# All AV runs of a batch behind its last scores, three row-tiled token blocks in the second GEMM, and a first GEMM that opens in the score banks

## The chip, the core and the metric

The kernel runs on one core of one Trainium2 chip. The metric is the time of one execution in device microseconds (us), and what is compared is the median of several executions. One further execution is recorded by the hardware profiler; all durations of single instructions come from that one.

## What is computed

A causal attention with forget gates, followed by an MLP with the exact GELU, both for 8 batches of 576 tokens with 8 heads of width 64. Cut to what matters:

```python
scores = q @ k.T / sqrt(64) + decay            # decay from cumsum(log f), causal mask
attn   = exp(scores - max); attn /= attn.sum(-1)
x      = (attn @ v)  -> [4608, 512]            # heads side by side
h      = x @ w_in                              # w_in  [512, 2048]
g      = 0.5 * h * (1 + erf(h / sqrt(2)))
out    = g @ w_out                             # w_out [2048, 512]
```

## The kernel before

The order of the work on every engine is written out by hand: each engine runs its instructions in the order in which the code issues them, and waits at an instruction for the semaphores of those on other engines. The waits themselves are placed by the framework, tile by tile: an instruction that writes a tile waits for the earlier readers of that tile.

**One batch.** A batch b from 2 to 7 is `attention(b)` (line 824) and then the rest of its first GEMM (lines 951 to 980). Its parts are these.

- Scores. For each of 4 head pairs i and each of 4 score tiles t, `scores(b, i, t)` (line 299) makes q times k for two heads at once. The matmuls have 64 rows of contraction, so the two heads run side by side in the two row halves of the array. ScalarE (ACT) takes the exponential of the tile from PSUM into an SBUF tile e (line 329), and GpSimd (POOL) masks the diagonal (line 331). The tiles t hold 448, 384, 448 and 320 columns for each head.
- Fill. Between the scores the PE works on the second GEMM of the batch before: `gemm2_rows` (line 489) is a generator of 64 steps, 16 for each of 4 blocks of 128 tokens, and `take(fill, n)` runs n of them. A step "n" is one matmul with 128 rows. A step "r" is row-tiled: two matmuls of 64 rows that run side by side, into two PSUM banks that VectorE (DVE) adds up later (a copy at line 517 and an addition at line 529, in `sum_out`). `PLAN` (line 472) says for each block which PSUM pool it takes and which steps are "r"; `FILL` (line 821) says how many steps follow each score tile.
- AV. `av(i)` (line 830) runs, for each of the two heads, 15 matmuls with 128 rows and 65 columns (line 350) into one bank of the pool "o", then `normalize` on DVE (a reciprocal at line 363 and a multiplication at line 364, from that bank into the SBUF tile x). When both heads are done, `x_dma` (line 388) has SyncE (SP) issue a DMA that transposes x into xT, the input of the first GEMM.
- First GEMM. `gemm1(b, ffb, kts, ps)` (line 400) adds the contraction parts kts (0 to 3, one for each head pair) of block ffb of 16 into the bank ps. With part 3 it issues `gelu`, an ACT instruction at line 425 that reads the bank.

**PSUM** has 8 banks: the pool "s" has two tiles of two banks each (the score tiles), "o" two tiles of one bank, "m" two tiles of one bank. Each pool hands its tiles out in turn.

**The order around the change**, for b of 3 to 7. `FILL` puts 7, 6, 3, 3 steps behind the four tiles of pair 0, and so on, 48 in the loop. `av(0)` and `av(1)` run inside the loop, behind the second tile of pairs 1 and 2 (line 842). After the loop come `av(2)`, 3 steps, `av(3)` with one step between its heads, the addition of block 2 that was put off (line 862), and the last 12 steps. Then the first GEMM opens:

```python
pss = [gemm1(b, ffb, (0, 1)) for ffb in range(2)]             # banks of "m"
for ffb in range(2):
    gemm1(b, ffb, (2,), pss[ffb])
pss += [gemm1(b, ffb, (0, 1, 2), spare()) for ffb in (2, 3)]  # banks of "o"
for ffb in range(4):
    gemm1(b, ffb, (3,), pss[ffb])                             # and a gelu each
more = s_psum.tile([P, 2, 512], FP32, tag="s", name="ps1")
gemm1(b, 4, ps=more[:, 0, :])
```

Blocks 5, 6 and 9 to 15 follow in banks of "m", blocks 7 and 8 in banks of "o". The other place where two blocks of the first GEMM share one tile of "s" is `gemm1_begin` (line 802), for batch 1; there the gelus of these two blocks are issued behind the last matmul of both (lines 814 to 817).

SP's queue of a batch holds, in this order: two transposing loads of the next batch's q and k, five loads of v, the store of token block 0, two more transposing loads, and then the `x_dma` of the four pairs with the stores of blocks 1 to 3 between and behind them.

Of the kernel before, what the change touches and what calls it, by code (L numbers as in the profile page):

```python
# [2 lines left out]

# [6 lines left out]
FP32 = mybir.dt.float32  # L10
# [5 lines left out]
P = 128  # L16
# [3 lines left out]
HP = 4  # L20
# [34 lines left out]
def kernel(  # L55
# [16 lines left out]
    n_ff = d_ff // P  # L72
# [11 lines left out]
    h_pool = ctx.enter_context(tc.tile_pool(name="h", bufs=1))  # L84
    e_pool = ctx.enter_context(tc.tile_pool(name="e", bufs=4))
    tq_pool = ctx.enter_context(tc.tile_pool(name="tq", bufs=1))
    x_pool = ctx.enter_context(tc.tile_pool(name="x", bufs=3))
    xT_pool = ctx.enter_context(tc.tile_pool(name="xT", bufs=2))
    g_pool = ctx.enter_context(tc.tile_pool(name="g", bufs=2))
    o_pool = ctx.enter_context(tc.tile_pool(name="outs", bufs=4))  # L90
    s_psum = ctx.enter_context(tc.tile_pool(name="s_psum", bufs=2, space=PSUM))
# [251 lines left out]
    def attend(b, i, h, ms, pool=o_psum, tag="o"):  # L343
        if (b, i, h) not in o_of:
            o_of[b, i, h] = pool.tile([P, NBLK, D + 1], FP32, tag=tag, name="o")
        o = o_of[b, i, h]
        for m in ms:
            for n in range(m + 1):
                t, c = where(n, m)
                nc.tensor.matmul(  # L350
                    o[:, m, :],
                    e_of[b, i, t][:, h, c : c + P],
                    vw_of[b][:, 2 * i + h, n, :],
                    start=(n == 0),
                    stop=(n == m),
                )

    def normalize(b, i, h):
        if (b, i) not in x_of:
            x_of[b, i] = x_pool.tile([P, NBLK, 2, D], BF16, tag="x", name="x")  # L360
        o = o_of[b, i, h]
        r = x_pool.tile([P, NBLK], FP32, tag="r", name="r")
        nc.vector.reciprocal(r, o[:, :, D])  # L363
        nc.vector.tensor_tensor(  # L364
            x_of[b, i][:, :, h, :],
            o[:, :, 0:D],
            r.unsqueeze(2).to_broadcast([P, NBLK, D]),
            Alu.mult,
        )

    def xT(b):
        if b not in xT_of:
            xT_of[b] = xT_pool.tile([P, n_dm, XC], BF16, tag="xT", name="xT")
        return xT_of[b]
# [25 lines left out]
    def gemm1(c, ffb, kts=range(4), ps=None, act=True):  # L400
        src = xT(c) if c < B else tails
        if ps is None:
            ps = m_psum.tile([P, TC], FP32, tag="m", name="ps1")
        for kt in kts:
            nc.tensor.matmul(  # L405
                ps,
                w_in_sb[:, kt, ffb * P : (ffb + 1) * P],
                src[:, kt, 0:TC],
                start=(kt == 0),
                stop=(kt == n_dm - 1),  # L410
            )
        if n_dm - 1 in kts and act:
            gelu(c, ffb, ps)
        return ps

    def spare():
        return o_psum.tile([P, TC], FP32, tag="o", name="ps1")

    def gelu(c, ffb, ps):
        if c not in g_of:  # L420
            g_of[c] = [
                g_pool.tile([P, TC], BF16, tag=f"g{n}", name=f"g{n}")
                for n in range(n_ff)
            ]
        nc.scalar.activation(g_of[c][ffb], ps, Act.Gelu)  # L425
# [9 lines left out]
    def gemm2(c):  # L435
# [35 lines left out]

    PLAN = [
        (0, "o", 16 * "r"),
        (1, "m", 6 * "r" + "n" + 7 * "r" + 2 * "n"),
        (2, "m", 16 * "r"),
        (3, "s", 16 * "n"),
    ]

    PLAN_0 = [(2, "o", 16 * "r"), (3, "m", 14 * "r" + 2 * "n")]
# [3 lines left out]
        (2, "m", 12 * "r" + 4 * "n"),  # L483
        (3, "s", 16 * "n"),
    ]

    put_off = []

    def gemm2_rows(c, plan):

        for ts, held, steps in plan:
            if held == "s":
                both = s_psum.tile([P, 2, d_model], FP32, tag="s", name="ps2")
                banks = [both[:, 0], both[:, 1]]
            else:
                pool = {"o": o_psum, "m": m_psum}[held]
                banks = [  # L500
                    pool.tile([P, d_model], FP32, tag=held, name="ps2")
                    for _ in range(2)
                ]
            ot = o_pool.tile([P, d_model], FP32, tag="ot", name="ot")
            for kt, step in enumerate(steps):
                last = kt == steps.rfind("r")
                for r in range(2 if step == "r" else 1):
                    rows = slice(r * D, (r + 1) * D) if step == "r" else slice(0, P)
                    nc.tensor.matmul(  # L509
                        banks[r],  # L510
                        g_of[c][kt][rows, ts * P : (ts + 1) * P],
                        w_out_sb[rows, kt, :],
                        start=kt == (steps.index("r") if r else 0),
                        stop=last if r else kt == n_ff - 1,
                    )
                if "r" in steps and (kt == n_ff - 1 if held == "s" else last):
                    nc.vector.tensor_copy(ot, banks[1])  # L517
                if kt == n_ff - 1:
                    if plan is PLAN and ts == 2:
                        put_off.append(partial(sum_out, c, ts, ot, banks[0]))  # L520
                    elif "r" in steps:
                        sum_out(c, ts, ot, banks[0])
                    else:
                        nc.vector.tensor_copy(ot, banks[0])
                        store(c, ts, ot)
                yield

# [53 lines left out]
    def gemm2_third():  # L581
        yield from gemm2_second(0)
        yield from gemm2_rows(0, PLAN_0)
        yield from gemm2_rows(1, PLAN_1)

    def take(gen, n):
        for _ in range(n):
            if next(gen, "end") == "end":
                return
# [228 lines left out]

    FILL = [[7, 6, 3, 3], [1, 3, 3, 3], [1, 2, 3, 3], [3, 2, 3, 2]]
    FILL_2 = [[8, 8, 8, 8], [8, 8, 4, 4], [4, 4, 4, 4], [4, 4, 4, 4]]

    def attention(b):


        fill = gemm2_third() if b == 2 else gemm2_rows(b - 1, PLAN)
        counts = FILL_2 if b == 2 else FILL

        def av(i, n=0):  # L830
            for h in range(2):
                attend(b, i, h, (0, 1, 2, 3, 4))
                normalize(b, i, h)
                if h == 0:
                    take(fill, n)
            x_dma(b, i)

        for i in range(HP):
            for t in range(4):
                scores(b, i, t)  # L840
                take(fill, counts[i][t])
                if t == 1 and 0 < i < (HP if b == 2 else HP - 1):
                    av(i - 1)
                    if b == 2 and i == 1:
                        load_v(3)
                if b == 2 and (i, t) == (0, 3):
                    weigh_v(b, 2)
                    weigh_v(b, 3)
                if b > 2 and i == 0 and t == 1:
                    load_v(b + 1)  # L850
                if b > 2 and t == 0 and i < 2:
                    transpose_dma(b + 1, 4 * i, 4 * i + 4)
                if b == 2 and t == 1 and i == 1:
                    transpose_dma(3, 0, 4)
        if b == 2:
            take(fill, 4)
            av(HP - 1)
        else:
            av(HP - 2)
            take(fill, 3)  # L860
            av(HP - 1, 1)
            put_off.pop()()
        take(fill, 4)
        if b == 2:
            transpose_dma(3, 4, 8)
        take(fill, 999)

        pss = [gemm1(b, ffb, (0, 1)) for ffb in range(2)]
        for ffb in range(2):
            gemm1(b, ffb, (2,), pss[ffb])  # L870
        pss += [gemm1(b, ffb, (0, 1, 2), spare()) for ffb in (2, 3)]
        for ffb in range(4):
            gemm1(b, ffb, (3,), pss[ffb])
        more = s_psum.tile([P, 2, 512], FP32, tag="s", name="ps1")
        gemm1(b, 4, ps=more[:, 0, :])
        if b + 1 < B:
            untangle(b + 1, 0)
            weigh_v(b + 1, 0)
        x_tail(b)
# [135 lines left out]
```

## Time and profile before

| | |
|---|---|
| median of 3 executions | 334.37 us (333.99 to 334.4) |
| the profiled execution | 335.58 us, of which the span of the profile is 333.8 us |
| PE (matmuls) busy | 325.1 us, 97% of the span |
| ACT busy | 205.5 us, 62% |
| DVE busy | 184.2 us, 55% |
| POOL busy | 134.2 us, 40% |
| DMA | 44.18 MB, mean 132 GB/s |
| batches 3 to 7 | 34.8 to 34.9 us each, of a span of 333.8 us |

The profile is of the one execution that has 335.58 us. PE means the matmuls and PEld the weight loads that run beside them. Matmuls are pipelined: the row of a 512-column matmul says 379 ns, but the next one starts some 216 ns after it. A group is named by line, engine, operation and tiles (out<-in), with the busy time and the mean time of one in ns. The chain of waits is the work that ended last, followed back from the end, each piece with its start and its length in us. The timeline gives start, length, engine, line and the number of instructions of a merged piece, and in brackets how long the engine was idle before it and for what it waited.

### The profile page before, as it was taken

What the parts mean: (1) busy time and instruction counts of PE and PEld (TensorE: products, weight loads), DVE (VectorE), ACT (ScalarE), POOL (GpSimd) and SP (SyncE); (2) the same over time, 40 slices, a digit from 0 to 9 for tenths busy, and PEclk for the clock granted to TensorE, in tenths of its full rate; (3) what the DMA queues carried; (4) which work ended last, traced back from release to release, by engine and by line L of the source; (5) the groups of instructions that cost most, each with busy time, mean ns of one, the idle gap of its engine ahead of it and who ended that gap; (6) DMA issues with size and microseconds to landing.
All of it is one profiled execution on the core that took longest, in us unless ns stands there. A gap on an engine that the chain in (4) does not pass through costs nothing.

```text
span 333.8 us, 8055 instructions
## 1 busy us (share of the span) xinstructions
PE 325.1 (97%) x3287; PEld 170.1 (51%) x3287; DVE 184.2 (55%) x427; ACT 205.5 (62%) x296; POOL 134.2 (40%) x260
## 2 busy tenths in 40 slices
PE   8899999999999999999999999999999999999995
PEld 4664555445554466445644565455544654444443
DVE  5852657474549855894589547954795450010011
ACT  4786886974535786478736892788278836405600
POOL 8897873039327054704472354534442420000000
PEclk9999999999999999999999999999999999999999
DMA  7899999989999899389939895889700420021022
GB/s 118 192 202 218 206 194 98 195 170 156 206 195 179 133 219 157 92 136 175 209 111 141 160 174 157 115 153 212 155 1 3 100 75 33 0 89 38 0 50 77
DMA packets 94948, 44.18 MB, mean 132 GB/s; under 512 B 74176, under 2 KB 89792, under 8 KB 94912
## 3 DMA queue, kind: packets, MB, share of 16 engines
q1 hardware_dynamic: 77760, 27.16, 42.6%
q0 software_dynamic: 16752, 15.99, 30.7%
q8 instruction: 25, 0.41, 0.5%
q10 hardware_dynamic: 400, 0.52, 0.4%
q14 instruction: 11, 0.09, 0.1%
HBM read 36.85 MB, written 9.44 MB: 139 GB/s over the span
## 4 chain that ended last, share of the span: by engine, by line
PE 95%; ACT 2%; DVE 1%; issue 1%; DVEq 0%
PE ps L405 37%; PE ps L509 27%; PE ps L449 8%; PE o L350 8%; PE s L319 7%; PE s L619 1%; PE ps_w L210 1%; PE ps_f L226 1%; ACT e L624 1%; PE ps L569 1%; PE ps L545 1%; PE o L650 0%; ACT e L329 0%; PE ps_x L383 0%; DVE x L664 0%
## 5 line engine op out<-in xcount | busy, mean ns | idle before, releaser
L425 ACT ACTIVATE g<-ps 128x512 bf16<-128x512 f32 x138 | 78.5, 602 | 79.5 <-PE ps L405 78.9
L405 PE MATMUL ps<-xT,w_in_sb 128*128 128x512 bf16 x512 | 114.1, 379 | 0.1
L509 PE MATMUL ps<-w_out_sb,g 64*128 64x512 bf16 (+1 forms) x711 | 108.5, 377 | 0.0
L329 ACT ACTIVATE e<-s 128x896 bf16<-128x896 f32 x112 | 87.7, 836 | 21.3 <-PE s L319 18.8
L405 PEld LDWEIGHTS <-w_in_sb 128*128 128x128 bf16 x576 | 55.3, 98 | 66.6 <-issue 2.6
L331 POOL TENSOR_SCALAR_AFFINE_SELECT e<-e 128x256 bf16<-128x256 bf16 (+1 forms) x135 | 49.1, 383 | 87.5 <-ACT e L329 87.1
L509 PEld LDWEIGHTS <-g 64*128 64x128 bf16 (+1 forms) x711 | 40.2, 95 | 34.8 <-issue 4.7
L288 POOL TENSOR_TENSOR vw<-v_sb,wT 128x640 bf16<-128x640 f32 (+1 forms) x30 | 38.3, 1278 | 26.1 <-PE s L319 16.2
L269 DVE COPY kT<-tk 64x288 bf16<-64x288 bf16 x96 | 46.1, 480 | 1.6
L269 DVE COPY qT<-tq 64x288 bf16<-64x288 bf16 x96 | 36.7, 383 | 5.8 <-DMA tq<-q 4.4
L517 DVE COPY ot<-ps 128x512 f32<-128x512 f32 x20 | 13.8, 691 | 47.2 <-PE ps L509 47.2
L319 PE MATMUL s<-qT,kT 64*128 64x256 bf16 (+2 forms) x336 | 37.6, 276 | 0.8 <-DVE kT L241 0.6
L350 PEld LDWEIGHTS <-e 128*128 128x128 bf16 x840 | 30.3, 98 | 7.9 <-POOL e L331 2.5
L458 DVE COPY ot<-ps 128x512 f32<-128x512 f32 (+2 forms) x9 | 5.7, 632 | 49.6 <-PE ps L449 49.6
L350 PE MATMUL o<-vw,e 128*128 128x65 bf16 x840 | 32.3, 194 | 0.0
L364 DVE TENSOR_TENSOR x<-o,r 128x320 bf16<-128x320 f32 x56 | 27.5, 492 | 3.2 <-DMA xT<-x 1.3
L449 PE MATMUL ps<-w_out_sb,g 128*128 128x512 bf16 (+2 forms) x144 | 28.0, 355 | 0.0
L319 PEld LDWEIGHTS <-kT 64*128 64x128 bf16 x336 | 16.9, 94 | 19.2 <-issue 4.2
L449 PEld LDWEIGHTS <-g 128*128 128x128 bf16 x144 | 13.5, 98 | 14.5
L529 DVE TENSOR_TENSOR ot<-ot,ps 128x512 f32<-128x512 f32 x22 | 15.1, 685 | 1.1
L363 DVE RECIPROCAL r<-o 128x5 f32<-128x5 f32 x56 | 10.5, 187 | 9.1 <-PE o L350 9.1
L405 PE MATMUL ps<-tails,w_in_sb 128*128 128x512 bf16 x64 | 14.3, 377 | 0.0
(89 smaller groups left out, 186.8 us busy)
## 6 DMA issues: line engine op xcount, KB each, us to landing
out_dram<-ot SPq DMA_DIRECT2D x32, 256.0 KB, 2.4
v_sb<-in_v_dram SPq DMA_DIRECT2D x24, 256.0 KB, 5.1
q<-in_q_dram POOLq DMA_DIRECT2D x6, 576.0 KB, 6.6
k<-in_k_dram POOLq DMA_DIRECT2D x6, 576.0 KB, 8.6
v_sb<-in_v_dram POOLq DMA_DIRECT2D x17, 128.0 KB, 6.5
w_in_sb<-in_moe_w_in_dram POOLq DMA_DIRECT2D x4, 512.0 KB, 7.2
w_out_sb<-in_moe_w_out_dram POOLq DMA_DIRECT2D x4, 512.0 KB, 9.4
v_sb<-in_v_dram SPq DMA_DIRECT2D x6, 128.0 KB, 4.6
```

What stands on the lines that cost most here:

```text
L269: nc.vector.tensor_copy(rows[:, odd], src[odd * D : (odd + 1) * D, 2 * i + h].rearrange("d j p -> d p j"),)
L288: eng.tensor_tensor(vw(b)[:, hs, n0:n1, 0:D], v_sb[:, hs, n0:n1, :], w.unsqueeze(3).to_broadcast([P, 2, n1 - n0, D]), Alu.mult,)
L319: nc.tensor.matmul(to, *ab, start=half < 0, stop=half == 1 or not masked)
L329: nc.scalar.activation(et[:, :, z:c], st[:, :, z:c], Act.Exp, scale=scale)
L331: nc.gpsimd.affine_select(out=et[:, :, c0 + z : c0 + P], in_=et[:, :, c0 + z : c0 + P], compare_op=Alu.is_ge, fill=0.0, base=z, pattern=[[ ...
L350: nc.tensor.matmul(o[:, m, :], e_of[b, i, t][:, h, c : c + P], vw_of[b][:, 2 * i + h, n, :], start=(n == 0), stop=(n == m),)
L364: nc.vector.tensor_tensor(x_of[b, i][:, :, h, :], o[:, :, 0:D], r.unsqueeze(2).to_broadcast([P, NBLK, D]), Alu.mult,)
L405: nc.tensor.matmul(ps, w_in_sb[:, kt, ffb * P : (ffb + 1) * P], src[:, kt, 0:TC], start=(kt == 0), stop=(kt == n_dm - 1),)
L425: nc.scalar.activation(g_of[c][ffb], ps, Act.Gelu)
L449: nc.tensor.matmul(pss[ts][:, c0:c1], g_of[c][kt][:, ts * P : (ts + 1) * P], w_out_sb[:, kt, c0:c1], start=(kt == 0), stop=(kt == n_ff - 1),)
L509: nc.tensor.matmul(banks[r], g_of[c][kt][rows, ts * P : (ts + 1) * P], w_out_sb[rows, kt, :], start=kt == (steps.index("r") if r else 0), ...
L529: nc.vector.tensor_tensor(ot, ot, bank, Alu.add)
```

## The change

For batches 3 to 7 (not for batch 2, whose branches keep the old order):

- `PLAN`: block 1 gets 16 "r" steps (13 "r" and 3 "n" before), block 2 moves from "m" to "o", and block 3 moves from "s" to "m" and opens with 4 "r" steps before 12 "n". So 52 of the 64 steps are row-tiled, and these are the first 52.
- For a block of 16 "r" steps the two banks change roles: the one that opened first is copied, the other is added (`banks.reverse()`). The addition of block 2 is no longer put off.
- `FILL` takes 52 steps in the loop (6, 4, 3, 3 for pair 0, then 3 each). No `av` runs in the loop. Behind it come `av(0)`, one step, `av(1)`, `av(2)` and `av(3)` with one step between the two heads of each, and the last 8 steps.
- The tiles x get 4 buffers in place of 3.
- Blocks 0 to 3 of the first GEMM take the four banks of two "s" tiles, blocks 0 and 1 the halves of one, blocks 2 and 3 those of the other. Block 4 goes to "m". The order of their matmuls stays the same, with each gelu still issued by `gemm1` right behind its block's part 3.

```diff
-    x_pool = ctx.enter_context(tc.tile_pool(name="x", bufs=3))
+    x_pool = ctx.enter_context(tc.tile_pool(name="x", bufs=4))
...
     PLAN = [
         (0, "o", 16 * "r"),
-        (1, "m", 6 * "r" + "n" + 7 * "r" + 2 * "n"),
-        (2, "m", 16 * "r"),
-        (3, "s", 16 * "n"),
+        (1, "m", 16 * "r"),
+        (2, "o", 16 * "r"),
+        (3, "m", 4 * "r" + 12 * "n"),
     ]
...
+                if plan is PLAN and last and kt == n_ff - 1:
+                    banks.reverse()
...
-                    if plan is PLAN and ts == 2:
-                        put_off.append(partial(sum_out, c, ts, ot, banks[0]))
-                    elif "r" in steps:
+                    if "r" in steps:
                         sum_out(c, ts, ot, banks[0])
...
-    FILL = [[7, 6, 3, 3], [1, 3, 3, 3], [1, 2, 3, 3], [3, 2, 3, 2]]
+    FILL = [[6, 4, 3, 3], [3, 3, 3, 3], [3, 3, 3, 3], [3, 3, 3, 3]]
...
-                if t == 1 and 0 < i < (HP if b == 2 else HP - 1):
+                if t == 1 and b == 2 and i > 0:
                     av(i - 1)
...
         else:
-            av(HP - 2)
-            take(fill, 3)
-            av(HP - 1, 1)
-            put_off.pop()()
+            av(0)
+            take(fill, 1)
+            for i in range(1, HP):
+                av(i, 1)
         take(fill, 4)
...
-        pss = [gemm1(b, ffb, (0, 1)) for ffb in range(2)]
+        if b == 2:
+            pss = [gemm1(b, ffb, (0, 1)) for ffb in range(2)]
+            pss += [spare(), spare()]
+        else:
+            pss = []
+            for _ in range(2):
+                wide = s_psum.tile([P, 2, 512], FP32, tag="s", name="ps1")
+                pss += [wide[:, 0, :], wide[:, 1, :]]
+            for ffb in range(2):
+                gemm1(b, ffb, (0, 1), pss[ffb])
         for ffb in range(2):
             gemm1(b, ffb, (2,), pss[ffb])
-        pss += [gemm1(b, ffb, (0, 1, 2), spare()) for ffb in (2, 3)]
+        for ffb in (2, 3):
+            gemm1(b, ffb, (0, 1, 2), pss[ffb])
         for ffb in range(4):
             gemm1(b, ffb, (3,), pss[ffb])
-        more = s_psum.tile([P, 2, 512], FP32, tag="s", name="ps1")
-        gemm1(b, 4, ps=more[:, 0, :])
+        if b == 2:
+            more = s_psum.tile([P, 2, 512], FP32, tag="s", name="ps1")
+            gemm1(b, 4, ps=more[:, 0, :])
+        else:
+            gemm1(b, 4)
```

More of the change, by code (lines that the diff above doesn't have):

```diff
@@ L1 @@
 from contextlib import ExitStack
-from functools import partial
 import concourse.bass as bass
@@ L485 @@
     ]
-    put_off = []
     def gemm2_rows(c, plan):
@@ L841, in attention @@
                 take(fill, counts[i][t])
-                if t == 1 and 0 < i < (HP if b == 2 else HP - 1):
+                if t == 1 and b == 2 and i > 0:
                     av(i - 1)
-                    if b == 2 and i == 1:
+                    if i == 1:
                         load_v(3)
```

## The prediction

> **What bounds the kernel now.** I read the busy times of the page first. PE is busy for 325.1 of 333.8 us; the next engine, ACT, for 62%.
>
> ```profile
> PE 325.1 (97%) x3287; PEld 170.1 (51%) x3287; DVE 184.2 (55%) x427; ACT 205.5 (62%) x296; POOL 134.2 (40%) x260
> ```
>
> Such a share is an average, so the table by windows came next, one window for each batch. In batch 4 (148.36 to 183.18) PE has no idle time at all and its clock is granted in full; batches 3, 5, 6 and 7 read the same.
>
> ```profile
> 148.36:183.18 34.82, 34.82 (x343) 18.35 (x343) 24.23 (x56) 23.99 (x34) 15.36 (x31) 1.00 0.88 153
> ```
>
> The waits of PE over batches 3 to 7 are none. So a batch is as long as its matmuls, and whatever PE comes to wait for is added in full. What PE loses today is seen only in the chain of waits of batch 4, in order of time (start, length, line):
>
> ```profile
> 148.42 0.30 PE s L319 x4
> ...
> 151.69 0.19 PE s L319 x2
> 151.88 0.65 PE ps L509 x6
> ...
> 153.89 0.75 PE ps L509 x5
> 154.64 0.95 PE o L350 x30
> 155.59 0.29 PE s L319 x2
> ...
> 163.97 1.06 PE o L350 x30
> ...
> 166.84 2.59 PE ps L509 x12
> ```
>
> A score of 448 columns takes 0.19, but 0.29 right behind an AV run; an AV run takes 0.95, but 1.06 behind 64-row matmuls. Each change between 64-row and 128-row matmuls costs about 0.10. Batch 4 has six: into the first score (148.42), into and out of the 128-row work around av(0) and av(1) (153.89, 155.59, 157.90, 159.38), and into av(2) (163.97).
>
> **What the change takes away.** Now the scores and the 52 row-tiled steps come first, then 128-row work to the end of the batch. Two changes are left of six: minus 4 x 0.10 = **-0.41 us** a batch. Seven more matmuls are issued (116 for 109 in the second GEMM), at no cost: three row-tiled steps (x6) take 0.65 and twelve plain ones 2.59, both 0.216 a step. The put-off addition, the fourth x buffer and the swapped banks cost nothing by themselves; what DVE then does is counted below. POOL's and DVE's work for the next batch is issued where it was.
>
> **New wait 1, the third score tile.** There are two score tiles, so the third score waits for the first exponential. That comes late at any rate: behind the last gelu and a table load.
>
> ```profile
> 148.46 0.60 ACT L425 ACTIVATE g<-ps 128x512 bf16<-128x512 f32 x1 [0.27 <-PE ps L405]
> 149.07 1.28 ACT L329 ACT_TABLE_LOAD   x1
> 150.37 4.88 ACT L329 ACTIVATE e<-s 128x896 bf16<-128x896 f32 x6
> ```
>
> The group of this shape has a mean of 918 ns, so it ends at 151.29. The hand-over from ACT to PE is 0.04, seen in batch 1, where PE did wait so:
>
> ```profile
> 45.60 1.52 ACT e L329 x2
> 47.12 0.04 issue
> 47.16 0.34 PE s L319 x4
> ```
>
> The third score may start at 151.33. Before, 7 and 6 steps covered this: PE's timeline has it at 151.53. With 6 and 4 it is three steps earlier, at 150.88, and waits **0.44**. Later tiles don't: four tiles with three steps each take PE 4 x 0.65 + 0.67 = 3.26, and ACT's four instructions (918, 805, 918 and 705 ns, less the overlap of one with the next, about 0.1) some 2.9. Ends of this cost: 0.20, the one wait of this kind in batch 1, and 0.65, all three steps. I take the sum from the batch's own rows.
>
> **New wait 2, the AV stretch.** There are two "o" banks, so the AV of a head waits until DVE has normalized the head two before. Spread out, this was free. The rows, from DVE's timeline in batch 4:
>
> ```profile
> 155.15 0.20 DVE L363 RECIPROCAL r<-o 128x5 f32<-128x5 f32 x1 [1.17 <-PE o L350]
> 155.38 0.49 DVE L364 TENSOR_TENSOR x<-o,r 128x320 bf16<-128x320 f32 x1
> 155.79 0.18 DVE L363 RECIPROCAL r<-o 128x5 f32<-128x5 f32 x1
> ```
>
> The head's first matmul is at 154.48, so 0.67 to the reciprocal, 0.72 to the end of the multiplication, and 0.15 from DVE to the next AV (batch 0's chain: 18.71 to 18.86). From av(i) to av(i+1), first head to first head, is thus 1.54, while PE has 2 x 0.475 + 0.216 = 1.17 of work there: 0.37 of waiting, for av(2) and av(3). For av(1) DVE is later, since the copy and addition of block 2 (0.73 apart) and the copy of block 3's row bank (0.61 behind each other in a full queue) stand ahead of the first reciprocal in its queue. With zero at the end of step 52: step 48 starts at -1.21 (five steps and a score), its copy starts at -0.81, the addition at -0.08, block 3's copy at 0.53, the reciprocal at 1.14, its head is free at 1.86, av(1) may start at 2.01. PE: change 0.10, first head 0.475, then 0.07 of waiting for the addition (which frees the second bank, at 0.65), second head to 1.12, one step to 1.34, wait 0.67. Sum 0.07 + 0.67 + 2 x 0.37 = **1.48**. With the 0.04 of ACT to PE in place of 0.15 it is 1.1; with 0.04 more at each of three hand-overs, 1.6.
>
> **New wait 3, the first GEMM in the score banks.** Blocks 0 and 1 now share one "s" tile, blocks 2 and 3 another. The order of the built program shows that part 3 of block 1 waits for ACT's gelu of block 0, and part 3 of block 3 for the gelu of block 2: reader and writer use different halves, but the waits go by tile. Behind the waiting matmul stands all of the first GEMM. ACT's timeline has the rows:
>
> ```profile
> 172.27 3.04 ACT L425 ACTIVATE g<-ps 128x512 bf16<-128x512 f32 x6 [6.52 <-PE ps L405]
> ```
>
> Part 3 of block 0 began at 171.86, so 0.41 to its gelu; one gelu takes 0.60, and in a full queue one follows another by 0.48. With T at part 3 of block 0: gelu to 1.01, block 1 at 1.05 in place of 0.22, wait 0.83. Block 2 at 1.27; its gelu stands behind that of block 1 (1.46), so 1.94 to 2.54; block 3 at 2.58 in place of 1.48, wait 1.10. Sum **1.93**; 1.86 without hand-overs, 2.2 with DVE's. Block 6 in "m" waits for the gelu of block 4, free by T+4.50; PE gets there at 4.53, no wait.
>
> **What is moved and stays hidden.** All four x_dma now stand together in SP's queue, behind the stores of blocks 0 to 2. SP needs 1.3 for one (three in 3.87 before), less than the 1.54 from av to av. The last x is ready at 7.17, landed 2.5 later (median of the landings) at 9.7; its part 3 is due at 10.57 (8 steps and 12 matmuls behind av(3)). Pair 2 lands at 8.1, due at 8.84. So the margin is 0.7 to 0.9, and this is free; an issue of 2.39 (the longest row) in place of 1.23 would cost 0.5.
>
> **Sum.** -0.41 + 0.44 + 1.48 + 1.93 = +3.44 a batch, five batches, **+17.2 us**. The profiled execution would go from 335.58 (span 333.8) to 352.8 (351.0). It lay 1.2 above the median, so the median goes from 334.37 to **351.6**.
>
> **A rule to weigh.** In the windows of 5 to 20 us, PE pauses of 0.5 to 1.2 us leave the granted clock at 1.00. The new pauses are no longer than 1.1, so I price the clock at nothing. The Trainium skill, "TensorE: Matmul & The Clock Gate", section "A second HAM failure mode: psum-queue depth-cycling", says otherwise: a PE that idles briefly again and again between groups, as it waits for PSUM, can drop to half its clock. By that page, one window of some 3.4 us at half speed a batch, an estimate, would be 1.7 more, 360 in all.
>
> **Rivals.**
> - *The half-tile wait doesn't bind.* Then -0.41 + 0.44 + 1.48, and block 6 waits 0.41 for the gelu of block 4 (2.96 + 0.04 against 2.59): +1.92 a batch, **344.0**. For it: the halves are different banks. Against it: the wait is in the program.
> - *The AV stretch is hidden* by a DVE that overlaps more than its rows show: -0.41 + 0.44 + 1.93 = +1.96, **344.2**. Against it: 1.54 is a chain of three dependent steps, not a rate.
> - *More is late*: x_dma queued behind stores, or the clock, **357 to 361**.
> - *Faster*: the changes of matmul height. Price 0.10 each, place the six pieces above. If the waits were all covered, -2.0 us, **332.3**. It decides only if a change were worth more than 3.85 / 4 = 0.96 us, or ACT and DVE kept 3.4 us a batch ahead of their rows; nothing in the chain points there.
> - *The change doesn't do what it says*: ruled out, as the built order has all 52 row-tiled steps ahead of the first AV.
>
> **Chances and range.** Forecast 0.80, half-tile rival 0.06, hidden AV 0.07, more late 0.04, faster or no change 0.03. The ends of the three waits and of x_dma give +2.75 (0.20 + 1.1 + 1.86) to +4.5 (0.65 + 1.6 + 2.2 + 0.5) a batch, 348.1 to 357; as all upper ends at once are unlikely, the range is 348.0 to 356.0, and it leaves out the rivals at 344. Slower by over 0.2% (what a measurement of this kernel can tell) 0.96, within 0.2% 0.01, faster 0.03.
>
> **What would show it.** Batches of about 38.3 in place of 34.8; in the waits, PE's first GEMM (L405 before) behind ACT's gelu ten times, 9.6 us in all; its scores behind the exponential five times, 2.2; AV behind DVE's multiplication, 7.4; two changes of height left in a batch; no wait of the first GEMM for xT. I am wrong if the first GEMM opens without a pause, or if AV heads follow each other at 1.17 a pair.

## The result, and the profile after

The changed kernel takes 354.0 us (median of 6 executions, 352.84 to 354.89); the kernel before, beside it on the same chip, takes 334.22 (median of 6). Medians, here and below, leave out single executions that lay over 1.5% above the fastest of the same kernel. The ratio is 1.057, with a 95% interval of 1.052 to 1.063. It is slower, as forecast, 2.4 above the predicted 351.6 and within its range of 348 to 356. The profiled execution of the changed kernel took 354.06, at its median, with a span of 352.4, which is 18.6 more than the 333.8 of before. (The profiled execution of before lay 1.4 above its median of these six; so the medians differ by 19.8 and the spans by 18.6. The working below goes by the spans.)

The page of the changed kernel: PE has as much work as before (325.1 there), but in a longer span.

```profile
PE 325.0 (92%) x3288; PEld 174.9 (50%) x3322; DVE 189.0 (54%) x432; ACT 208.0 (59%) x296; POOL 134.2 (38%) x260
```

The table by windows, one window a batch, here batches 4 and 5 (columns: window, its length, busy time and instructions of PE, PEld, DVE, ACT, POOL, granted clock, DMA share, GB/s):

```profile
152.15:191.28 39.13, 35.31 (x347) 19.49 (x350) 25.14 (x56) 24.42 (x34) 15.37 (x31) 1.00 0.79 138
191.28:229.58 38.30, 35.15 (x346) 19.50 (x349) 25.08 (x56) 24.43 (x34) 15.20 (x31) 1.00 0.74 134
```

Before, batch 4 was 34.82 long with PE busy for 34.82. Now PE is idle for 3.15 us of batch 5 and 3.8 of batch 4. The same view gives 38.31 for batch 6 and 38.88 for batch 3; the granted clock is 1.00 in all windows of batches 3 to 7. So batches 5 and 6 agree within 0.01, and batches 3 and 4 are 0.57 and 0.82 longer; that difference was not forecast. No score follows batch 7, so its length is taken to the end of its first GEMM, where the last second GEMM starts: 38.38 (267.89 to 306.27), and 34.72 before (252.96 to 287.69). That is 3.66 more, 0.17 above the 3.49 of batches 5 and 6 (38.31 against 34.82).

PE's waits over batches 3 to 7 (line waited at, what ended the wait: us in total, times, the longest). Before there were none.

```profile
PE ps L404 <- ACT g L424: 8.2, 10, 1.0
PE o L349 <- DVE r L362: 3.4, 5, 0.7
PE o L349 <- DVE x L363: 2.1, 10, 0.2
PE s L318 <- ACT e L328: 1.5, 5, 0.4
PE ps L404 <- DMA xT<-x: 1.0, 2, 0.7
```

The view counts idle time after the modelled end of the last matmul; from start to start each of these waits is up to 0.2 longer. The first line is the first GEMM behind the gelus, the second and third the AV stretch, the fourth the third score tile: the three waits of the prediction, ten, fifteen and five times, so twice, three times and once a batch. The last line is a fourth that the prediction had priced at nothing. It counts batches 3 and 4; batch 7 has a third one, too short for the view: its first GEMM starts at 290.32 and stops for 0.17 before 291.36, just behind the landing of the third transpose at 291.32.

The chain of waits in batch 4 shows all four in order (start, length, line):

```profile
154.16 0.93 ACT e L328
155.13 0.36 PE s L318 x2
...
167.98 0.49 DVE x L363
168.62 0.65 PE o L349 x15
...
169.52 0.50 DVE x L363
170.16 0.65 PE o L349 x15
...
172.27 3.96 DMA xT<-x
176.27 2.12 PE ps L404 x9
178.41 0.61 ACT g L424
179.06 0.39 PE ps L404
179.47 1.09 ACT g L424 x2
180.61 2.53 PE ps L404 x11
```

Where before had only PE's lines, one score now starts behind an exponential (155.13), one AV run behind a normalization (168.62, 170.16; they are 1.54 apart), the first GEMM behind a transposed x (176.27), and its parts 3 behind the gelus (179.06, 180.61).

### The profile page after: what moved, and what is told of

It reads as the page before. It is cut to its first block, busy times and chain, and to the rows that moved or that the text cites. A ratio compares the mean times of both kernels' runs of the same rounds, so it can differ in the third digit from the quotient of the medians.

```text
span 352.4 us, 8113 instructions
## 1 busy us (share of the span) xinstructions
PE 325.0 (92%) x3288; PEld 174.9 (50%) x3322; DVE 189.0 (54%) x432; ACT 208.0 (59%) x296; POOL 134.2 (38%) x260
## 4 chain that ended last, share of the span: by engine, by line
PE 72%; DMA 9%; ACT 7%; DVE 5%; issue 3%; POOL 3%; DVEq 0%; POOLq 0%; ACTq 0%
PE ps L404 32%; PE ps L506 19%; PE ps L448 8%; PE o L349 5%; PE s L318 5%; ACT g L424 3%; DMA q<-in_k_dram 3%; DMA k<-in_k_dram 2%; DMA xT<-x 2%; DVE x L363 2%; ACT e L328 2%; ACT L328 2%; DMA v_sb<-in_v_dram 2%; DVE ot L516 1%; DVE r L362 1%
## 5 line engine op out<-in xcount | busy, mean ns | idle before, releaser
L424 ACT ACTIVATE g<-ps 128x512 bf16<-128x512 f32 x138 | 80.6, 598 | 102.7 <-PE ps L404 102.2
L506 PE MATMUL ps<-w_out_sb,g 64*128 64x512 bf16 (+1 forms) x732 | 105.1, 376 | 0.5 <-issue 0.5
L506 PEld LDWEIGHTS <-g 64*128 64x128 bf16 (+1 forms) x746 | 42.6, 94 | 29.8 <-issue 1.3
L516 DVE COPY ot<-ps 128x512 f32<-128x512 f32 x25 | 17.3, 690 | 64.3 <-PE ps L506 64.3
L268 DVE COPY kT<-tk 64x288 bf16<-64x288 bf16 x96 | 43.0, 448 | 4.7 <-DMA tk<-k 3.0
L268 DVE COPY qT<-tq 64x288 bf16<-64x288 bf16 x96 | 39.8, 415 | 1.5
L318 PE MATMUL s<-qT,kT 64*128 64x256 bf16 (+1 forms) x336 | 37.8, 275 | 2.4 <-ACT e L328 1.7
L349 PE MATMUL o<-vw,e 128*128 128x65 bf16 x840 | 34.5, 194 | 5.8 <-DVE r L362 3.4
L526 DVE TENSOR_TENSOR ot<-ot,ps 128x512 f32<-128x512 f32 x27 | 18.6, 688 | 7.0 <-PE ps L506 5.0
L621 ACT ACTIVATE e<-s 128x1024 bf16<-128x1024 f32 (+1 forms) x13 | 12.1, 991 | 1.8 <-PE s L616 1.6
```

Source lines behind the costliest of these rows:

```text
L268: nc.vector.tensor_copy(rows[:, odd], src[odd * D : (odd + 1) * D, 2 * i + h].rearrange("d j p -> d p j"),)
L318: nc.tensor.matmul(to, *ab, start=half < 0, stop=half == 1 or not masked)
L349: nc.tensor.matmul(o[:, m, :], e_of[b, i, t][:, h, c : c + P], vw_of[b][:, 2 * i + h, n, :], start=(n == 0), stop=(n == m),)
L506: nc.tensor.matmul(banks[r], g_of[c][kt][rows, ts * P : (ts + 1) * P], w_out_sb[rows, kt, :], start=kt == (steps.index("r") if r else 0), ...
```

## The experiments

The theory was the prediction's: three separate waits, each with its own cause (the tile that two blocks share, the two banks of "o", the number of steps behind the first two score tiles), that add up, plus a gain of 0.4 from fewer changes of matmul height. Each run takes away one cause. Two rivals had to be told apart: that the waits overlap, so that taking one away only bares the next, and, for the unforecast wait, whether a transpose of x is late by chance, by its queue, or by something in the program.

The periods (first score to first score, us) are those of the profiled executions, one for each kernel:

| kernel | median us | ratio to before, 95% | batch 3 | 4 | 5 | 6 |
|---|---|---|---|---|---|---|
| before | 334.2 to 334.6 | 1 | 34.82 | 34.82 | 34.96 | 34.82 |
| after | 354.0 | 1.052 to 1.063 | 38.88 | 39.13 | 38.30 | 38.31 |
| e1_gelus_behind | 347.21 | 1.029 to 1.047 | 37.39 | 38.24 | 36.99 | 36.99 |
| e2_gelus_behind_o | 343.84 | 1.018 to 1.036 | 36.72 | 36.96 | 36.35 | 36.35 |
| e3_fill | 351.33 | 1.041 to 1.060 | 38.30 | 39.09 | 37.89 | 37.89 |
| e4_av_in_loop | 357.23 | 1.058 to 1.074 | 39.08 | 39.92 | 39.02 | 39.02 |
| e5_open_o_m | 344.09 | 1.025 to 1.030 | 36.73 | 37.10 | 36.35 | 36.34 |
| e6_steps_in_av | 352.96 | 1.053 to 1.060 | 38.66 | 39.05 | 37.70 | 37.91 |
| e7_av_four_banks | 340.75 | 1.015 to 1.021 | 36.04 | 36.81 | 35.20 | 36.46 |
| e8_shift | 354.33 | 1.056 to 1.068 | 38.63 | 38.31 | 38.30 | 39.09 |
| e9_best | 334.50 | 0.996 to 1.003 | 35.05 | 35.15 | 34.43 | 34.65 |
| e10_act_copy | 334.18 | 0.997 to 1.003 | 34.80 | 34.52 | 34.43 | 34.61 |
| e11_act_copy_parts | 333.03 | 0.995 to 1.001 | 34.43 | 34.51 | 34.43 | 34.43 |
| e12_parts | 334.25 | 0.997 to 1.003 | 34.84 | 34.67 | 34.43 | 34.62 |

### The shared score tile: e1, e2, e5

e1 keeps the score banks, but issues the gelus of two blocks behind part 3 of both:

```diff
         for ffb in range(4):
-            gemm1(b, ffb, (3,), pss[ffb])
+            gemm1(b, ffb, (3,), pss[ffb], b == 2)
+            if b > 2 and ffb % 2:
+                gelu(b, ffb - 1, pss[ffb - 1])
+                gelu(b, ffb, pss[ffb])
```

> The changed kernel, but with the gelus of the two blocks that share a score tile issued behind part 3 of both. Theory (the two waits of part 3 for a gelu are the price of a shared tile): the waits of 0.85 and 1.12 a batch go, but the first gelu starts 0.2 later and so block 6 has to wait for the gelu of block 4, 0.6 a batch. Net -1.3 a batch, -6.6 in all: 347.4 us against 354.0. Rival (the pause at the opening comes from xT landing late, or from ACT reading a bank beside the one that PE writes): the pause stays where it is, 354.

Measured: 347.21. The two waits of a batch are gone and the third one that was foreseen has come, while the lines of the AV stretch and of the scores read as in the changed kernel; the other two of PE's waits in e1:

```profile
PE ps L404 <- ACT g L424: 2.4, 5, 0.5
...
PE ps L404 <- DMA xT<-x: 1.6, 3, 1.1
```

The line of the gelus now counts 5 in place of 10: block 6, which takes the bank of block 4. e2 is e1 with blocks 6 and 7 in "o", where blocks 7 and 8 were:

```diff
-            aside = ffb in (7, 8) if b > 1 else b == 1 and ffb % 4 < 2
+            aside = ffb in ((7, 8) if b == 2 else (6, 7)) if b > 1 else b == 1 and ffb % 4 < 2
```

> As the kernel with the gelus behind both matmuls, and blocks 6 and 7 in the banks of o, block 8 in m, so that block 6 doesn't wait for the gelu of block 4. Theory: no wait for a gelu is left in the first GEMM, -1.95 a batch, -9.8 in all: 344.2 us. Rival (block 6 never waited, ACT's rows overlap more than I count): the same as the kernel without this edit, about 344 for both.

Measured: 343.84, and no wait for a gelu left; batches 5 and 6 take 36.35, 1.95 less than in the changed kernel. e5 gets there by other banks, with each gelu where the change put it: blocks 0 and 1 open in "o", 2 and 3 in "m", 4 in half a score tile, 5 and 6 in "o".

```diff
-            pss = []
-            for _ in range(2):
-                wide = s_psum.tile([P, 2, 512], FP32, tag="s", name="ps1")
-                pss += [wide[:, 0, :], wide[:, 1, :]]
-            for ffb in range(2):
-                gemm1(b, ffb, (0, 1), pss[ffb])
+            pss = [gemm1(b, ffb, (0, 1), spare()) for ffb in range(2)]
```

> The changed kernel with the first GEMM opened in four single banks: blocks 0 and 1 in o, 2 and 3 in m, block 4 in half a score tile, blocks 5 and 6 in o. The gelus stay right behind their blocks. Theory (the price is the tile that two blocks share, not the order of the gelus): the waits of PE for a gelu go without a gelu moved, -1.95 a batch, as with the gelus behind both and block 6 in o (343.8): 344 us. Rival (the early gelus themselves hold PE up, by their reads of PSUM beside its writes): some pause stays, 348 or more.

Measured: 344.09, the same periods of 36.35. So the cause is the tile that two blocks share, not the number of gelus or their place as such. The rival that the half-tile wait doesn't bind has fallen: it is 1.95 to 1.97 a batch.

### The third score tile: e3

```diff
-    FILL = [[6, 4, 3, 3], [3, 3, 3, 3], [3, 3, 3, 3], [3, 3, 3, 3]]
+    FILL = [[7, 6, 3, 3], [3, 3, 3, 2], [3, 3, 3, 2], [3, 3, 3, 2]]
```

> The changed kernel with 7 and 6 steps behind the first two score tiles, as before the change, and 2 for 3 behind the last tile of each later pair: still 52. Theory: the wait of the third score tile for the first exponential (0.46 a batch) goes and no later tile waits, since ACT needs 2.9 us for four tiles and PE has 3.04: -2.2 in all, 351.8 us. Rival (ACT is the limit of the score stage, so a wait taken away here comes back at a later tile): no change, 354.

Measured: 351.33. The wait of the scores for the exponential is no longer in the view, and batches 5 and 6 are 0.41 and 0.42 shorter. Three steps more behind the first two tiles cover the exponential; their place elsewhere cost nothing.

### The AV stretch: e4, e6, e7

e4 puts av(0) and av(1) back into the loop and leaves the rest of the change. For that the steps are dealt out so that block 1 is closed where av(1) stands:

```diff
-    FILL = [[6, 4, 3, 3], [3, 3, 3, 3], [3, 3, 3, 3], [3, 3, 3, 3]]
+    FILL = [[6, 4, 3, 3], [3, 3, 3, 3], [2, 2, 4, 4], [3, 3, 3, 3]]
...
-                if t == 1 and b == 2 and i > 0:
+                if t == 1 and 0 < i < (HP if b == 2 else HP - 1):
                     av(i - 1)
...
-            av(0)
-            take(fill, 1)
-            for i in range(1, HP):
-                av(i, 1)
+            av(HP - 2)
+            take(fill, 3)
+            av(HP - 1, 1)
```

> The changed kernel with av(0) and av(1) back in the loop and av(2), three steps, av(3) behind it, as before the change; one step more is moved behind the second tile of pair 2 so that block 2 opens its banks of o behind av(1). PLAN and the opening of the first GEMM stay changed. Theory: the four changes between 64 and 128 rows come back (+0.41 a batch), the waits of AV for DVE go from 1.51 to about 0.3, and the x_dma of the first two pairs go out early, so that the waits for xT (1.35 in all) go too: -4 to -5.4 in all, 348.6 to 350. Rival (the changes of height cost more than 0.10, so that one stretch pays for its waits): 354 or more.

Measured: 357.23, slower than the change itself; the expectation missed by 7 or more. The new line among PE's waits in e4:

```profile
PE ps L506 <- DVE x L363: 5.5, 10, 0.9
```

No line of AV is left in that view, as expected, but the second GEMM (L506) now waits for DVE, twice a batch, next to the gelus and the exponential as before. The chain in batch 4 says why:

```profile
162.08 0.69 DVE ot L516
...
163.70 0.49 DVE x L363
...
164.32 0.50 DVE x L363
164.87 1.93 PE ps L506 x15
```

Block 2 of the second GEMM opens right behind av(1), in the two "o" banks that this AV has just filled, and its first step waits until DVE has copied, added and normalized. In the kernel before, block 2 was in "m". So the place of AV and the bank of block 2 belong together: the change can put block 2 into "o" only because no AV runs in the loop. From start to start the new wait is 1.44 in batch 5, and the four changes of height that come back are 0.4; against them stand the 1.51 of AV waits that went. That makes about half of the 0.71 by which batch 5 of e4 is longer than in the changed kernel; the other half was not followed further.

e6 leaves AV in its stretch and moves steps from behind it into it, so that PE has work while DVE normalizes:

```diff
             av(0)
-            take(fill, 1)
-            for i in range(1, HP):
-                av(i, 1)
+            take(fill, 4)
+            av(1, 1)
+            take(fill, 2)
+            av(2, 1)
+            take(fill, 2)
+            av(3, 1)
```

> The changed kernel with seven of the last eight steps moved into the AV stretch, three more behind av(0), two more each behind av(1) and av(2). Theory: PE now has work where it waited for DVE, so the 1.5 us a batch of waiting in AV go; but the last x is ready no sooner and the first GEMM comes 1.4 to 1.5 sooner, so part 2 waits some 0.75 for xT, where the margin was 0.78. Net -0.75 a batch, about -3.8 in all: 350 us, with waits of the first GEMM for xT in all five batches. Rival (the AV stretch is bound by DVE's rate, not by two banks): the waits in AV stay, 354.

Measured: 352.96, 1.0 less than the changed kernel, where 3.8 had been expected. The AV waits are gone from the view, but most of the time is given back one stage later: batches 3 to 6 together are 1.3 shorter, for 6.0 of AV waits (4 x 1.51). The line of PE's waits that grew in e6:

```profile
PE ps L404 <- DMA xT<-x: 5.9, 5, 2.0
```

Before the edit 8 steps stood between the last AV and the first GEMM, and now one; 7 x 0.216 = 1.5 us of cover for the transposes of x is gone, and now every batch waits for them. The wait for DVE and the wait for x are two faces of one chain: normalization, issue, landing.

e7 takes the cause away instead: with the banks of e5, the heads of the odd pairs go into the score tiles, which are free by then, so that four banks serve the stretch.

```diff
-            o_of[b, i, h] = pool.tile([P, NBLK, D + 1], FP32, tag=tag, name="o")
+            if b > 2 and i % 2:
+                wide = s_psum.tile([P, 2, 512], FP32, tag="s", name="o")
+                o_of[b, i, h] = wide[:, 0, 0 : NBLK * (D + 1)].rearrange(
+                    "p (n c) -> p n c", n=NBLK
+                )
+            else:
+                o_of[b, i, h] = pool.tile([P, NBLK, D + 1], FP32, tag=tag, name="o")
```

> The kernel with the first GEMM opened in single banks, and besides the AV runs of pairs 1 and 3 in a score tile for each head, which stand idle by then: four banks for AV in place of two. Theory (AV waits because a head needs the bank of the head two before): the waits in AV go but for 0.14 at av(0), -1.37 a batch against the kernel with single banks, less a wait for xT of 0.1 to 0.3 and the late transfers of one or two batches: -5 to -6.5, 337.5 to 339 us. Rival (DVE's rate of 0.63 us a head is the limit): the waits move to later heads or to xT in full, 343 to 344.

Measured: 340.75. Batch 5, the only one in which no transpose of x was late, takes 35.20, 1.15 less than in e5. Beside the scores' wait for the exponential, which this run leaves in, the view of e7 has one line only, the first GEMM behind x:

```profile
PE ps L410 <- DMA xT<-x: 4.1, 6, 1.7
```

Batch 5 has a wait for x too, of 0.23 from start to start and too short for this view. Its third transpose is on time (2.40), but the faster AV stretch has used up the margin, as the expectation had it (0.1 to 0.3). The chain of waits there (start, length, line):

```profile
204.75 2.40 DMA xT<-x
207.15 0.04 issue
207.19 2.97 PE ps L410 x13
```

With these 0.23 and the 0.14 that stay ahead of av(0)'s second head, the 1.15 make up the 1.51 of AV waits. Batches 3, 4 and 6 lost 0.8 to 1.6 more to late transposes. After e6 this was the second time that whatever was gained ahead of the first GEMM bared xT.

### What makes a transpose of x late: e8

Of the 24 transposes of x in each trace half or more land 2.4 to 2.7 after their issue, the others later, up to 5.7. The DMA view of the changed kernel in batch 4, around the late ones (172.2 to 176.3), first, and in batch 5 around punctual ones (211.6 to 214.1), second:

```profile
q8 instruction: 1, 0.02, 1.6%
...
xT<-x SPq DMA_TRANSPOSE x2, 3.5
```

```profile
q1 hardware_dynamic: 1328, 0.32, 57.6%
...
xT<-x SPq DMA_TRANSPOSE x2, 2.4
```

The first stretch holds a packet of the queue "instruction", the second has none. The page of the changed kernel counts 26 such packets in 0.43 MB, about 16 KB each, where the trace has 6,635 rows on PE: on average one for about 256 of PE's instructions. The theory is that these are the fetches of PE's program, and that a transpose under way then is held up by them. If so, a shift of the program against the batches moves the late batches. e8 issues 65 more small warm-up matmuls at the start, which add nothing to the output:

```diff
-        warm_up(9)
+        warm_up(2)
+        warm_up(72, D)
```

> The changed kernel with 65 more matmuls of PE at the very start: 2 warm-up matmuls of 512 columns and 72 of 64 columns for the 9 of 512, so the start takes about as long; 130 more instructions in PE's stream. In the changed kernel the transposes of x land 2.4 after their issue, but 3 to 4.3 where a 16 KB packet of the queue called instruction falls into their time, and such packets come every 256 PE instructions or so. Theory (the waits for xT in batches 3 and 4, 1.35 in all, come from PE's instruction fetches): with the stream shifted the packets of batches 3 and 4 fall on pair 0, which has time, and one falls on pairs 1 and 2 of batch 5: no wait for xT in batches 3 and 4, one of 0.3 to 0.9 in batch 5; 353 to 354 us. Rival (the late transfers come from other traffic of these two batches): the waits stay in batches 3 and 4.

Measured: 354.33. Batch 3 is down to 38.63 and batch 4 to 38.31, and batch 6 is at 39.09, where it had been 38.31. PE's one wait for x:

```profile
PE ps L404 <- DMA xT<-x: 0.6, 1, 0.6
```

The fetch of that stretch is at 251.19, and the third transpose of batch 6 lands 3.92 after its issue. The expectation named batch 5. There the second transpose did land late (3.96) and the third after 2.79, but PE needed neither sooner; the wait came one batch later. Batch 3 still waits 0.27 from start to start, too short for the view: its first transpose is late (3.20) and the ones behind it in the queue are issued late. So the wait of batch 4 is gone, that of batch 3 is halved, and batch 6 has a new one: the wait moves with PE's program and is tied to no batch. A shift in time alone does not move it: in e1, e2, e3 and e5, where batch 3 begins anywhere from 112.15 to 113.74 and PE's program is as long as in the changed kernel within 5 rows, the waits for x are in batches 3 and 4 and not in 5 and 6, as there. Over the 14 traces of this study the count is clear: of 152 transposes with such a packet between issue and landing 132 took over 2.7, of 184 without one only 4.

### A version without the waits: e9 to e12

e9 puts together the denser first tiles of e3 and the four AV banks of e7, av(0) with one step between its heads, and opens the first GEMM with six blocks in six single banks, so that 24 matmuls in place of 16 give the transposes time:

```diff
+            pss = [gemm1(b, ffb, (0, 1), spare()) for ffb in range(2)]
+            for ffb in (2, 3):
+                one = s_psum.tile([P, 2, 512], FP32, tag="s", name="ps1")
+                pss.append(gemm1(b, ffb, (0, 1), one[:, 0, :]))
+            pss += [gemm1(b, ffb, (0, 1)) for ffb in (4, 5)]
+            for k in (2, 3):
+                for ffb in range(6):
+                    gemm1(b, ffb, (k,), pss[ffb])
...
+            aside = ffb in ((7, 8) if b == 2 else (6, 7, 10, 11)) if b > 1 else b == 1 and ffb % 4 < 2
```

> The changed kernel with all its new waits taken away: 7 and 6 steps behind the first two score tiles; AV in four banks, with one step between the heads of av(0) too; and a first GEMM that opens with parts 0 and 1, then part 2, then part 3 of six blocks in six single banks (two of o, half of each score tile, two of m), so that xT of pair 2 is due 12 matmuls and that of pair 3 is due 18 matmuls behind the last step, in place of 4 and 12; blocks 6, 7, 10, 11 in o. Theory (three waits and xT behind them are all that the change costs, and four changes of height all that it gains): no wait of PE but where a late transpose falls on pair 3, so batches of 34.4 us, 0.41 under the 34.8 of before: -2.0 in all, 332.4 us against 334.4 before, 0.6% faster. Rival (the changes of height that are gone come back elsewhere, or DVE's rate shows when all else is cured): batches of 34.8 or more, 334.4 us or above.

Measured: 334.50, 2.1 above the expectation, and no different from before (0.996 to 1.003). Batch 5 takes 34.43: 0.39 less than before (0.41 had been worked out for the four changes of height). The others take 0.62, 0.72 and 0.22 more than that, again for x. DVE's timeline in batch 4 of e9 shows what sets the issue of the transposes:

```profile
161.64 0.69 DVE L522 COPY ot<-ps 128x512 f32<-128x512 f32 x1 [3.03 <-PE ps L512]
162.44 0.69 DVE L532 TENSOR_TENSOR ot<-ot,ps 128x512 f32<-128x512 f32 x1
163.04 0.68 DVE L522 COPY ot<-ps 128x512 f32<-128x512 f32 x1
163.64 0.18 DVE L368 RECIPROCAL r<-o 128x5 f32<-128x5 f32 x1
...
168.25 0.49 DVE L369 TENSOR_TENSOR x<-o,r 128x320 bf16<-128x320 f32 x1
```

No line but the first has a bracket with idle time ahead of it: DVE works through from 161.64 to 168.74. e10 hands the copy at 163.04, of block 3's row bank, to ACT, which is between its exponentials and gelus then:

```diff
-                    nc.vector.tensor_copy(ot, banks[1])
+                    copy = nc.scalar.copy if plan is PLAN and ts == 3 else nc.vector.tensor_copy
+                    copy(ot, banks[1])
```

> The kernel of the run with four AV banks, the denser first tiles and six opening blocks (e9), with one copy moved: the first half of the fourth token block's sum (512 columns, 0.69 us on DVE) goes to ACT, which has nothing to do in the AV stretch. In e9 DVE works without a pause from the copies of the third token block (161.64 in batch 4) to the last normalization (168.74), with this copy (163.04 to 163.73) between them, so by my theory DVE sets when the transposes of x are issued. Then all four are issued 0.6 to 0.7 earlier against PE's work, and the waits of the first GEMM for x (0.62 in batch 3, 0.72 in batch 4, 0.22 in batch 6 by the batch periods, 1.56 in all) shrink to 0 to 0.2: 333.0 to 333.2 and periods of 34.43 to 34.6. Rival: the issue of the transposes is set by PE's own AV order (15 instructions a head and a step a pair), DVE only follows; then nothing moves and the time stays at 334.5.

e11 is e10 with the opening part by part (part 0 of all six blocks, then part 1, 2 and 3), and e12 has this order alone, with the copy on DVE:

```diff
-            pss = [gemm1(b, ffb, (0, 1), spare()) for ffb in range(2)]
+            pss = [gemm1(b, ffb, (0,), spare()) for ffb in range(2)]
...
-            for k in (2, 3):
+            for k in (1, 2, 3):
```

> As e10, and the opening of the first GEMM goes part by part through its six blocks (part 0 of all six, then part 1, 2, 3) and not parts 0 and 1 of each block together, so that the second transpose of x is needed 5 instructions (1.08 us) later; no work is added. If a late second pair is still waited for in e10, this takes it: 333.0. If the waits of e10 were all for the third pair, both give the same time, within 0.2. Rival: each of the six banks now opens 0.22 after the one before instead of 0.43, and banks held by the fourth token block's sum or by the last exponentials come late: 0.2 to 0.5 a batch, 334 to 335.5.

> The kernel with four AV banks, the denser first tiles and six opening blocks (e9), with the opening of the first GEMM part by part as in e11, and the copy back on DVE as in e9. It tells which of e11's two edits took the waits for x, and whether the copy on ACT is what lengthened the time outside the span (1.7 in e9, 2.4 in e10 and e11). By my theory a second or first pair that a fetch delays is then covered, and a delayed third pair is not: the wait of batch 4 (third pair in e9, 0.72) stays, those of batches 3 and 6 (0.62, 0.22) go if the fetches fall on the first two pairs again: 333.5 to 333.9, with 1.7 outside the span. Rival, that DVE's copy is what counts and the order nothing: 334.3 to 334.6, with periods of 35.0 in batches 3 and 4.

Measured: the waits for x, by the periods of batches 3 to 6 over 34.43, are 1.56 in e9, 0.64 in e10, 0.84 in e12, and 0.08 in e11. To the end of its first GEMM batch 7 takes 34.77, 35.25, 34.92 and 34.33 in the same order. Counted over the 34.33, that makes the sums of five batches 2.00, 1.56, 1.43 and 0.08. So each of the two edits alone takes a fifth to a little over a quarter of the waits, both together nearly all. How much each is worth by itself one trace can't say, since the fetches fall on other transposes in each run. That both count shows in single batches: in e10 the first transpose of batch 4 is issued 16.37 behind the first score, in e9 16.60, so DVE does not only follow; and in batch 7 of e10 the second transpose lands 4.05 after its issue and PE waits 0.92 for it, while in e11 it lands after 4.02 and PE does not wait. Neither rival (DVE only follows; the order is nothing) holds. The window of batch 5 in e11:

```profile
180.58:215.01 34.43, 34.43 (x350) 18.60 (x350) 24.30 (x56) 24.14 (x35) 15.38 (x31) 1.00 0.84 156
```

PE is busy throughout again, 0.39 below the 34.82 of before. The medians: e10 334.18 (333.0 to 333.2 expected), e12 334.25 (333.5 to 333.9 expected), e11 333.03 (333.0 expected, 334.41 for before beside it). In e10 and e11 the time outside the span is 2.4 (median), in e9 and e12 1.7 and in before 1.8: the copy on ACT costs 0.6 to 0.7 there, for a reason that the traces, which begin with the span, don't show. Against the five batches of before (174.14 with its batch 7 of 34.72), those of e9, e10, e11 and e12 are 0.09, 0.53, 2.01 and 0.66 shorter. With 0.6 more outside the span for e10 and e11 this makes -0.1, +0.1, -1.4 and -0.7; the medians differ from those of before beside them by 0.0, -0.2, -1.4 and -0.4. Within 0.3 the batches thus account for the medians; what is left is less than what the start alone varies by from one execution to the next (the first score of batch 3 lies between 111.64 and 114.0 in the profiles of this study). The interval of e11, 0.995 to 1.001, just takes in no change: it is the fastest of all kernels here by its median, and not proven to be faster than before.

## Why the prediction was right, point by point

- **Changes of matmul height, -0.41.** e11 has the same order of heights as the changed kernel and almost no wait: 34.43 in place of 34.82, so -0.39. Right.
- **Third score tile, +0.44.** 0.46 from start to start; 0.41 gained in e3. Right.
- **AV stretch, +1.48.** 1.51: 0.14 ahead of the second head of av(0) (0.07 in the prediction), 0.63 ahead of av(1) (0.67), 0.37 ahead of av(2) and of av(3) (0.37). The distance from av to av was 1.54, as worked out from DVE's three rows and the hand-over. With four banks in place of two, e7 gained 1.15 in the one batch in which no x was late; 0.14 of the 1.51 stay there (the second bank still waits for the addition of block 2), and 0.23 came back as a wait for a transpose that was on time. The rival that DVE overlaps more than its rows show has fallen.
- **First GEMM in the score banks, +1.93.** 1.97 (0.85 and 1.12, forecast 0.83 and 1.10); 1.95 gained in e2 and e5. Right, and by the cause named: the wait goes by tile, though reader and writer use different banks.
- **Transposes of x, 0.** This term was mis-sized. "So the margin is 0.7 to 0.9, and this is free" took the median landing, 2.5. The trace of before already held landings of over 2.7, 7 of its 24; a landing of 4.0 in place of 2.5 eats the margin and 0.6 to 0.8 more. It happened in three batches of five: 0.57 + 0.82 + 0.17 = 1.56. The bound that the prediction kept for it, a longer issue, was another mechanism and 0.5 a batch. One wait of this kind, 0.14 in batch 5 of before, goes off again.
- **The sum.** 5 x 3.49 (batches 5 and 6 against 34.82) + 1.56 - 0.14 = 18.9, less 0.26 because batch 3 began that much earlier (113.27 for 113.53): 18.6, as measured in the span; forecast 17.2. The late transposes make most of the difference, the 3.49 of a batch in place of 3.44 about 0.3 of it. The median is off by 2.4 and not by 1.4 because the forecast took the changed kernel's profiled execution to lie 1.2 above the median, as that of before did; it lay at it.
- **The clock.** Granted at 1.00 in all five windows, through pauses of up to 1.1 several times a batch. The row was the better guide here; the drop to half the clock after short, repeated waits for PSUM of which the Trainium skill tells ("TensorE: Matmul & The Clock Gate", section "A second HAM failure mode: psum-queue depth-cycling"), and by which it would have been some 360, did not show in any window.
- **The rival on the other side.** It was said that the changes of height would be worth 2.0 if all waits were covered. e11 is that kernel: -2.0 in the five batches. So the change has a gain in it, as large as forecast, and pays for it some ten times over in waits (0.46 + 1.51 + 1.97 = 3.94 a batch against 0.39).

## What to carry to other kernels

Before work is moved together to save small costs on the busiest engine, list for each engine behind it how long it takes per piece and how many buffers lie between: eight AV runs in a row are paced by DVE's chain of 1.54 a pair, not by PE's 1.17. Two banks in one tile are one buffer to whoever waits by tile; where a reader starts while the other half is still being written, give each half a tile of its own, or let all readers come behind all writers. A margin for a transfer is to be held against its slow landings in the trace, not against its median, and work that is moved out from behind the producer takes away that margin (e6 gave back most of what it gained).

## What the runs showed of the hardware

A transposing DMA of x lands late in these traces when a packet of the queue "instruction" falls into its time: mostly 2.7 to 5.7 us after its issue in place of 2.4 to 2.6 (132 of 152 with a packet took over 2.7, 4 of 184 without). The packets are of about 16 KB and come about once in 256 instructions of PE, so they are taken here for the fetches of PE's program. An edit at the start of a kernel can thus lengthen a batch in its middle: 65 more matmuls, which do nothing else, moved 0.8 us from batch 4 to batch 6 (e8). That it is the fetch itself that holds up the transpose, and by what part of the DMA engines, was not tried by itself.

A copy on ACT, five in the whole program, went with 0.6 to 0.7 us more outside the span (e10, e11 against e9, e12). Its cause is open.
